# Linear attention and two FFNs on one core: the projected keys of pairs 9 to 13, with each head's rounded keys and their rest stacked on 128 rows

## The chip, the cores and the metric

One core of one Trainium2 chip runs the whole program. The metric is the device time of one execution in microseconds (us); a kernel's time is the median of its runs.

Engines are named as in the profile: PE is TensorE, PEld its weight load, DVE VectorE, ACT ScalarE, POOL GpSimd and SP SyncE, which here only issues transfers. SPq is SP's queue.

## The reference

```python
def phi(x):
    proj = np.einsum('bhsd,df->bhsf', x, w_phi)
    proj = proj - np.max(np.abs(proj), axis=-1, keepdims=True)
    return np.concatenate([np.exp(proj), np.exp(-proj)], axis=-1)
q_p, k_p = (phi(q), phi(k))
kv = np.einsum('bhsf,bhsd->bhfd', k_p, v)
z = np.sum(k_p, axis=2)
num = np.einsum('bhsf,bhfd->bhsd', q_p, kv)
den = np.einsum('bhsf,bhf->bhs', q_p, z)[..., None] + 1e-06
x = num / den                                # then heads side by side: 2304 x 512
h = x @ w_in1; x = np.maximum(0.01 * h, h) @ w_out1
h = x @ w_in2; x = (h / (1 + np.exp(-h))) @ w_out2
```

There are 4 x 8 = 32 heads, 576 positions each, head size 64 and 128 projected features. All data are fp32. The FFNs go from 512 to 2048 and back, for 2304 tokens.

## The kernel before, in words

**Pairs.** Two heads of one batch are one pair, so there are 16 pairs. A head has 64 rows, and a pair's raw keys (`kr`, 128 x 512) hold head 0 on rows 0 to 63 and head 1 on rows 64 to 127; the last 64 positions of both heads lie in `kt`. `full(i)` is true of pairs 0 to 7, which project in fp32. Pairs 8 to 15 take the split path: a value is rounded to the type F32R ("h"), what the rounding left is a second F32R value (the rest, "l"), and a product is built of passes with h and l parts. `sub(l, x, h)` is a DVE subtraction that gives the rest; all its uses carry line L271 in the profile.

**Steps of a split pair**, one function each: `s_split` rounds keys and queries; `s_pk(0)` and `s_pk(1)` project the keys, two chunks of 128 positions each into one PSUM bank; `s_pkt` projects the last 64 positions; `s_pq(a)` projects half of the queries; `s_eq(a)` and `k_exp` take the exponentials; `s_kv` sums keys times values (L389, L394) and splits the result into `KVH` and `KVL`; `num_split(a)` forms numerator and denominator (L576, copied to SBUF as `x` by ACT at L577), and sends the denominator through DRAM (`rec`) to be spread over 64 rows; `s_fin(a)` multiplies (L595) and splits the result for the FFN (L416).

A chunk of `s_pk` takes three passes of 256 columns, both heads side by side in the block-diagonal weights: L322 (rounded keys by rounded weights `BDH`), L323 (rest of keys by `BDH`), L324 (rounded keys by the weights' rest `BDL`). They add up in PSUM. `k_sub` then takes the largest magnitude of each group of 128 features (L299) and subtracts it (L300), both from PSUM.

**Around them** runs the first FFN for tokens that are ready: L851 multiplies into h, `g` (L857) and `gh` (L862) are its activation and rounding on ACT, `gl` the rest on DVE, and L882 multiplies them by `wo`, 12 passes a tile (8 with `gh`, 4 with `gl`). Jobs that prepare the second FFN's weights (`w7s`, `wst`) are put between.

**What sets the order.** Pairs 0 to 7 follow a table of times. A step of pair i from 8 on is emitted at 8 units times (i - 8) plus its entry in `OFF1`; `EARLY` gives hand-set times for pair 8 and a few steps of pair 9. Emission order gives priorities, by which a scheduler writes one list for each engine and each DMA queue; a list is worked off in order. PSUM tiles come from two pools of four banks each, `ps_a` and `ps_y`. All key and query projections, `kv`, `num` and h take a bank from `ps_a` in turn, so a pass waits until the bank's last tile has been read.

Of the kernel before, what the change touches and what calls it, by code (L numbers as in the profile page):

```python
# [102 lines left out]
EARLY = {  # L103
    (8, "lq"): (117.29,),
    (8, "lv"): (117.39,),
    (8, "sp"): (123.8, 127.98, 131.89, 133.51, 137.47, 140.31, 142.48, 147.66),
    (9, "lq"): (151.8,),
    (8, "pq0"): (161.92, 162.63),
    (8, "eq0"): (165.65, 167.79, 171.38, 172.55, 173.81),
# [12 lines left out]
def tile_linear_attention_ffn_ffn(ctx: ExitStack, tc: tile.TileContext, q, k, v, w_phi, w_in1, w_out1, w_in2, w_out2, out):  # L122


    nc = tc.nc
# [8 lines left out]
    HALF = S // 2  # L134
    WOB = 3
    RAWB = 3
    NFULL = 8
    ABUFS0 = dict(kr=2, kt=2, qr=3, va=3, ke=2, p=2, m=2, qh=2, x=2)
    ABUFS1 = dict(kr=2, kt=2, qr=2, va=1, qh=2, ql=2, x=2, d=2)
    NKV, NNUM = 128, 128  # L140
    MIN64, MAX64 = 2.0**-15, 122872.0

# [72 lines left out]
    WH = attc.tile([128, F], F32R, name="WH")  # L215
    BDH = attc.tile([128, 2, F], F32R, name="BDH")
    BDL = attc.tile([128, 2, F], F32R, name="BDL")

    def make_consts():
        for c in (slice(0, 2 * F), slice(2 * F, 3 * F + 128)):  # L220
# [32 lines left out]
    def load_qk(i):  # L253

        st = P[i]
        st["kr"] = at([128, S0], F32, "kr")
        st["kt"] = at([128, 128], F32, "kt")
        st["qr"] = at([128, S], F32, "qr")
        for c in (slice(0, 256), slice(256, S0)) if i == 0 else (slice(0, S0),):
            nc.sync.dma_start(st["kr"][:, c], k[i, :, c])  # L260
        nc.sync.dma_start(st["kt"], k[i, :, S0:])
        nc.sync.dma_start(st["qr"], q[i])

    def load_v(i):

# [4 lines left out]
    def sub(out_, x, h):  # L270
        return nc.vector.tensor_tensor(out_, x, h.bitcast(F32), op=ALU.subtract)  # L271
# [4 lines left out]
    def s_split(i):  # L276

        st = P[i]
        h, l = at([128, S0], F32R, "krh"), at([128, S0], F32R, "krl")
        nc.scalar.activation(h, st["kr"], AF.Copy)  # L280
        sub(l, st["kr"], h)
        st["krh"], st["krl"] = h, l
        qs = at([128, 2, S], F32R, "qs")
        for j in range(2):
            r, o = (slice(0, 64), slice(64, 128))[:: 1 - 2 * j]
            nc.scalar.activation(qs[r, j], st["qr"][r], AF.Copy)
            sub(qs[o, j], st["qr"][r], qs[r, j])
        st["qs"] = qs
        t = at([128, 128], F32R, "kth")
        nc.scalar.activation(t, st["kt"], AF.Copy)  # L290
        sub(t[64:128], st["kt"][64:128], t[64:128])
        st["kth"] = t

    def k_sub(i, pk, ng, g0):

        ke = P[i]["ke"]
        km = at([128, 4], F32, "km")
        src = pk[:, 0 : ng * F].rearrange("p (g f) -> p g f", f=F)
        nc.vector.tensor_reduce(km[:, 0:ng], src, op=ALU.max, axis=AX.X, apply_absolute_value=True)  # L299
        nc.vector.tensor_tensor(  # L300
            ke[:, g0 : g0 + ng, 0, :], src, km[:, 0:ng].unsqueeze(2).to_broadcast([128, ng, F]), op=ALU.subtract
        )

    def k_exp(i, g0, g1):
# [3 lines left out]
        nc.scalar.activation(e1, e0, AF.Exp, scale=-1.0)  # L308
        nc.scalar.activation(e0, e0, AF.Exp)

    def s_pk(c2):
        def f(i):
            st = P[i]
            if c2 == 0:
                st["ke"] = at([128, 9, 2, F], F32, "ke")
            pk = ps("a")
# [12 lines left out]
        return f  # L329
# [14 lines left out]
    def s_pq(a):  # L344

        def f(i):
            st = P[i]
            c0, n = part(i, a)
            p = at([128, 2 * n], F32, "p")
            st["p", a] = p  # L350
            pq = [ps("a"), ps("a")]
            cs = slice(c0, c0 + n)
            for j in range(2):
                nc.tensor.matmul(pq[j][:, 0:n], WH, st["qs"][:, j, cs], start=True, stop=False)
                nc.tensor.matmul(pq[j][:, 0:n], BDL[:, j], st["qs"][:, j, cs], start=False, stop=True)
# [210 lines left out]
    def num_split(i, a):  # L566
# [4 lines left out]
        for j in range(2):  # L571
            o = pn[j][:, 0:w]
            todo = [(s, g, m) for s in range(2) for g, m in (("KVH", "qh"), ("KVH", "ql"), ("KVL", "qh"))]
            for n, (s, g, m) in enumerate(todo):
                lhs = st[g][:, j, s].rearrange("p t d -> p (t d)")
# [37 lines left out]
    OFF1 = dict(lv=0.6, lq=-2.1250, sp=0.5, pq0=2.1172, pk0=4.0606, pk1=4.0616, pq1=4.7479, eq0=6.2094, pkt=5.1, kv=8.3898, num0=12.1423, eq1=13.9119, num1=14.457, fin0=FIN, fin1=FIN + 2.3)  # L613
# [729 lines left out]
def layout(inputs):  # L1343
# [16 lines left out]
    for j in range(2):  # L1360
        r = slice(64 * j, 64 * j + 64)
        va[:, r, 8 + j, D] = 1
        va[:, r, 8 + j, :D] = vp[:, j, S0:]

    bd = np.zeros((2 * D, 2 * w_phi.shape[1]), w_phi.dtype)
    for j in range(2):
        bd[D * j : D * j + D, w_phi.shape[1] * j : w_phi.shape[1] * (j + 1)] = w_phi
# [37 lines left out]
```

## Time and profile before

| | |
|---|---|
| median of 3 runs | 930.43 us (929.99 to 930.52) |
| profiled execution, its time | 930.31 us |
| profiled execution, its span | 928.5 us |
| PE busy | 922.0 us (99%) |
| DVE busy | 699.4 us (75%) |
| ACT busy | 600.8 us (65%) |
| POOL busy | 110.7 us (12%) |
| granted TensorE clock | 1.00 |

The span runs from the first to the last instruction that the profiler saw; 1.8 us of the execution's own time lie around it. Busy times of PE overlap with one another, because a pass starts before the one ahead has drained: what a pass costs is read from the start of one to the start of the next.

### The profile page before, as it was taken

Reading aid. Unit: us, or ns where it says so; the run is one execution under the profiler, and the core shown is the slowest. Engines: PE = TensorE matmul, PEld = TensorE weight load, DVE = VectorE, ACT = ScalarE, POOL = GpSimd, SP = SyncE. Lnnn points to the kernel's source line nnn. Section 1 sums busy time; section 2 is a strip of 40 time slices with the busy share of each in tenths; the row PEclk is TensorE's granted clock in tenths of the full one; section 3 lists DMA queues with packets and bytes.
Section 4 is the critical chain, followed back from the end, with each engine's and each line's share of the span. In section 5 each row is a group of like instructions: output and inputs, shape, how many; then the busy total and the mean of one; then the engine's idle time right before and its main releaser. Section 6 shows DMA issues by size and latency. Waiting matters only on the chain.

```text
span 928.5 us, 15779 instructions
## 1 busy us (share of the span) xinstructions
PE 922.0 (99%) x5382; PEld 873.1 (94%) x5382; DVE 699.4 (75%) x1425; ACT 600.8 (65%) x1240; POOL 110.7 (12%) x110
## 2 busy tenths in 40 slices
PE   8999999999999999999999999999999999999998
PEld 7999989999999999988988899999999999999998
DVE  6889999967777775799998888889755377553754
ACT  6888787876766665565767657766645456454553
POOL 4443000111211110101111111111000000000000
PEclk9999999999999999999999999999999999999999
DMA  6854474463434631569867899999898678977784
GB/s 230 277 187 171 139 253 158 158 209 122 124 122 131 210 107 59 203 248 335 314 238 268 296 371 364 381 360 353 280 364 269 221 243 289 317 259 227 245 271 162
DMA packets 99647, 221.40 MB, mean 238 GB/s; under 512 B 14896, under 2 KB 25264, under 8 KB 99568
## 3 DMA queue, kind: packets, MB, share of 16 engines
q1 hardware_dynamic: 90496, 187.79, 60.2%
q0 software_dynamic: 8640, 32.25, 9.1%
q8 instruction: 43, 0.70, 0.3%
q10 hardware_dynamic: 432, 0.36, 0.1%
q14 instruction: 36, 0.29, 0.1%
HBM read 173.10 MB, written 47.22 MB: 237 GB/s over the span
## 4 chain that ended last, share of the span: by engine, by line
PE 95%; ACT 1%; DVE 1%; DMA 1%; issue 1%; POOL 0%; SPq 0%; POOLq 0%; ACTq 0%; DVEq 0%
PE ps_y L1163 19%; PE ps_y L882 16%; PE ps_a L851 13%; PE ps_y L1080 10%; PE ps_a L1080 10%; PE ps_a L991 6%; PE ps_a L394 5%; PE ps_a L882 4%; PE ps_a L576 3%; PE ps_a L525 2%; PE ps_y L394 1%; PE ps_y L525 1%; DMA w7s<-wst 1%; PE ps_a L389 1%; DMA qr<-in_q_dram 0%
## 5 line engine op out<-in xcount | busy, mean ns | idle before, releaser
L1163 PE MATMUL ps_y<-gt,ws 128*128 128x384 f32 x1008 | 178.2, 337 | 0.0
L1163 PEld LDWEIGHTS ps_y<-gt,ws 128*128 128x128 f32 x1008 | 176.4, 188 | 1.0 <-DVE gt L271 0.7
L851 PE MATMUL ps_a<-xh,wi 128*128 128x462 f32 (+1 forms) x384 | 119.0, 373 | 0.0
L882 PE MATMUL ps_y<-gh,wo 128*128 128x462 f32 (+1 forms) x440 | 102.5, 372 | 0.0
L1080 PE MATMUL ps_y<-xs,ws 128*128 128x384 f32 x504 | 97.6, 338 | 0.0
L1080 PE MATMUL ps_a<-xs,ws 128*128 128x384 f32 x504 | 96.0, 338 | 0.0
L701 ACT ACTIVATE gt<-g 128x384 fp32r<-128x384 f32 x120 | 62.3, 524 | 46.1 <-PE ps_y L1163 44.8
L882 PEld LDWEIGHTS ps_y<-gh,wo 128*128 128x128 f32 x440 | 81.9, 188 | 9.0
L1080 PEld LDWEIGHTS ps_y<-xs,ws 128*128 128x128 f32 x504 | 89.5, 188 | 0.3
L1080 PEld LDWEIGHTS ps_a<-xs,ws 128*128 128x128 f32 x504 | 89.2, 188 | 0.0
L271 DVE TENSOR_TENSOR gt<-g,gt 128x384 fp32r<-128x384 f32 x120 | 65.1, 555 | 30.9 <-ACT gt L701 30.3
L851 PEld LDWEIGHTS ps_a<-xh,wi 128*128 128x128 f32 x384 | 72.1, 188 | 7.7
L851 PE MATMUL ps_a<-xl,wi 128*128 128x462 f32 (+1 forms) x192 | 71.4, 372 | 0.0
L1055 DVE TENSOR_TENSOR g<-ps_a,hs 128x384 f32<-128x384 f32 x36 | 20.0, 556 | 59.5 <-PE ps_a L1080 59.4
L359 POOL PARTITION_ALL_REDUCE m<-p x16 | 36.1, 2256 | 228.4 <-ACT p L357 176.1
L731 POOL DMA_DIRECT2D w7s<-wst x60 | 32.5, 542 | 233.2 <-DVE wst L271 162.7
L882 PE MATMUL ps_y<-gl,wo 128*128 128x462 f32 (+1 forms) x220 | 56.1, 374 | 0.0
L1051 ACT ACTIVATE hs<-ps_y 128x384 f32<-128x384 f32 x54 | 26.3, 487 | 35.7 <-DVE g L1055 33.2
L271 DVE TENSOR_TENSOR gl<-g,gh 128x462 fp32r<-128x462 f32 (+1 forms) x64 | 40.5, 633 | 10.8 <-ACT gh L862 9.6
L394 PE MATMUL ps_a<-va,ke 128*128 128x128 f32 x384 | 46.9, 275 | 0.0
L687 DVE CUSTOM_DVE_ANT_0 r<-t,r 128x1024 uint16<-128x1024 uint16 x64 | 45.3, 713 | 0.8
L882 PEld LDWEIGHTS ps_y<-gl,wo 128*128 128x128 f32 x220 | 41.0, 188 | 4.6
(215 smaller groups left out, 1956.6 us busy)
## 6 DMA issues: line engine op xcount, KB each, us to landing
ws<-w7s SPq DMA_DIRECT2D x336, 256.0 KB, 4.2
wo<-wos SPq DMA_DIRECT2D x46, 512.0 KB, 4.1
w7s<-wst POOLq DMA_DIRECT2D x45, 512.0 KB, 5.4
raw<-in_moe_w_out_dram SPq DMA_DIRECT2D x32, 512.0 KB, 5.0
rawi<-in_moe_w_in_dram SPq DMA_DIRECT2D x16, 512.0 KB, 6.3
wos<-wo SPq DMA_DIRECT2D x16, 512.0 KB, 2.9
raw<-in_moe_w_in_dram SPq DMA_DIRECT2D x16, 512.0 KB, 5.4
va<-in_v_dram SPq DMA_DIRECT2D x16, 325.0 KB, 4.8
```

Source lines behind the costliest of these rows:

```text
L271: return nc.vector.tensor_tensor(out_, x, h.bitcast(F32), op=ALU.subtract)
L359: nc.gpsimd.partition_all_reduce(m, p, 128, bass_isa.ReduceOp.absmax)
L394: nc.tensor.matmul(pv[:, s, j], ke[:, g, s, :], vf[:, w : w + NKV], start=False, stop=(j == 1 and c == 3), skip_group_check=True)
L525: nc.tensor.matmul(pb[:, w : w + NNUM], e[:, s, cs], KV[:, s, j], start=(s == 0), stop=(s == 1))
L687: nc.vector.tensor_tensor(r, t.bitcast(U32), r, op=ALU.add)
L701: nc.scalar.activation(h, f, AF.Copy)
L731: (nc.sync if seq else nc.gpsimd).dma_start(w7s[m_, p, :, i : i + m], o.bitcast(F32))
L851: nc.tensor.matmul(ph, a[:, kk, :], b_[:, kk, :], start=(m == 0), stop=(m == 3 * KD - 1))
L882: nc.tensor.matmul(Y[t][d][:, 0:n], a[:, ds_], b_, start=(c == 0 and m == 0), stop=(c == NC - 1 and m == 1), skip_group_check=True)
L991: nc.tensor.matmul(bank[b_], w1_of(p, wi_, a, kk), x1_of(xi, c, kk), start=(first and m == 0), stop=(m == 5), skip_group_check=True)
L1080: nc.tensor.matmul(bank[b_], w[:, a, kk], x[:, c, kk], start=(first and m == 0), stop=(m == 5), skip_group_check=True)
L1163: nc.tensor.matmul(bank[b_][db], w[:, a, db], t[:, c], start=(first and p_ == 0 and m == 0), stop=(p_ == NP - 1 and m == 2), skip_group_ch ...
```

## The change

For pairs 9 to 13 (`STACK`) the host lays out each head's keys twice, on rows 0 to 63 and again on rows 64 to 127, and the queries of pairs 8 to 15 likewise. One ACT copy rounds all 128 rows, and one DVE subtraction turns rows 64 to 127 into the rest. One pass over 128 rows then multiplies (rounded, rest) of one head and one chunk by `WB[:, 0:2]`, 256 columns: the first 128 are the rounded weights on both row halves and give the main sum, the others are the weights' rest on rows 0 to 63 and zero below, and give the correction. A chunk so takes two passes, one a head, and a bank of its own. ACT copies the correction half to SBUF, DVE adds the main half to it, and `k_sub` works on the sum in SBUF.

The other edits: queries are rounded for both heads at once; `KVH` and `KVL` are laid out by sign first and filled by two copies and two subtractions instead of four and four; `kr` and `qr` have one buffer instead of two; `pk0`, `pk1` and `pkt` have earlier entries in `OFF1`; `EARLY` loses two entries.

```diff
-    (8, "sp"): (123.8, 127.98, 131.89, 133.51, 137.47, 140.31, 142.48, 147.66),
+    (8, "sp"): (123.8, 127.98, 131.89, 137.47, 142.48, 147.66),
...
-    NFULL = 8
+    NFULL, STACK = 8, range(9, 14)
...
-    ABUFS1 = dict(kr=2, kt=2, qr=2, va=1, qh=2, ql=2, x=2, d=2)
+    ABUFS1 = dict(kr=1, kt=2, qr=1, va=1, qh=2, ql=2, x=2, d=2)
...
-        st["kr"] = at([128, S0], F32, "kr")
+        st["kr"] = at([128, S0] if i not in STACK else [128, 2, S0], F32, "kr")
...
-        st["qr"] = at([128, S], F32, "qr")
+        st["qr"] = at([128, S] if full(i) else [128, 2, S], F32, "qr")
...
+            nc.sync.dma_start(st["kr"], k[row : row + 2, :, 0:S0].rearrange("j p s -> p j s"))
...
-        h, l = at([128, S0], F32R, "krh"), at([128, S0], F32R, "krl")
-        nc.scalar.activation(h, st["kr"], AF.Copy)
-        sub(l, st["kr"], h)
-        st["krh"], st["krl"] = h, l
+        st["krs"] = at([128, 2, S0], F32R, "krs")
+        if i not in STACK:
+            h, l = st["krh"], st["krl"] = st["krs"][:, 0], st["krs"][:, 1]
+            nc.scalar.activation(h, st["kr"], AF.Copy)
+            sub(l, st["kr"], h)
+        else:
+            h = st["krs"]
+            nc.scalar.activation(h, st["kr"], AF.Copy)
+            sub(h[64:128], st["kr"][64:128], h[64:128])
         qs = at([128, 2, S], F32R, "qs")
-        for j in range(2):
-            r, o = (slice(0, 64), slice(64, 128))[:: 1 - 2 * j]
-            nc.scalar.activation(qs[r, j], st["qr"][r], AF.Copy)
-            sub(qs[o, j], st["qr"][r], qs[r, j])
+        nc.scalar.activation(qs, st["qr"], AF.Copy)
+        sub(qs[64:128], st["qr"][64:128], qs[64:128])
...
+    def stacked(i, c2):
+        st = P[i]
+        ke = st["ke"]
+        for c in (2 * c2, 2 * c2 + 1):
+            pk = ps("a").rearrange("p (t j f) -> p t j f", t=2, j=2)
+            for j in range(2):
+                nc.tensor.matmul(pk[:, :, j], st["krs"][:, j, c * 128 : (c + 1) * 128], WB[:, 0:2].rearrange("p t f -> p (t f)"), start=True, stop=True)
+            x, y = (ke[:, 2 * c : 2 * c + 2, t] for t in range(2))
+            nc.scalar.activation(y, pk[:, 1], AF.Copy)
+            nc.vector.tensor_tensor(x, pk[:, 0], y, op=ALU.add)
+        x = ke[:, 4 * c2 : 4 * c2 + 4, 0]
+        k_sub(i, x, 4, 4 * c2)
+        if c2 == 0:
+            k_exp(i, 0, 4)
...
-        for j in range(2):
-            kv_, z_ = pv[:, :, j, 0:D], pv[:, :, j, D : D + 1].to_broadcast([128, 2, D])
-            for slot, sr in ((j, kv_), (1 - j, z_)):
-                ops = nc.scalar.activation(h[:, j, :, slot, :], sr, AF.Copy), sub(l[:, j, :, slot, :], sr, h[:, j, :, slot, :])
+        z_ = pv[:, :, :, D : D + 1].to_broadcast([128, 2, 2, D])
+        for slots, sr in ((slice(0, 4, 3), pv[:, :, :, 0:D]), (slice(1, 3), z_)):
+            ho, lo = (x.rearrange("p s j t d -> p s (j t) d")[:, :, slots] for x in (h, l))
+            ops = nc.scalar.activation(ho, sr, AF.Copy), sub(lo, sr, ho)
...
-    OFF1 = dict(..., pk0=4.0606, pk1=4.0616, ..., pkt=5.1, ...)
+    OFF1 = dict(..., pk0=3.2, pk1=3.9, ..., pkt=4.6, ...)
```

In the order of TensorE's instructions, this stood at the key projection of pair 11 before (a tile's name, then what it is computed from; the group of three passes follows three more times, and then L576):

```order
L882 MATMUL ps_y<-gh,wo_2676 128x462 x8
L882 MATMUL ps_y<-gl,wo_2676 128x462 x4
L322 MATMUL ps_a<-BDH,krh 128x256
L323 MATMUL ps_a<-BDH,krl 128x256
L324 MATMUL ps_a<-BDL,krh 128x256
L322 MATMUL ps_a<-BDH,krh 128x256
```

And this stands there now (L908 is the line that was L882, L325 is the stacked pass):

```order
L908 MATMUL ps_y<-gl,wo_2670 128x462
L325 MATMUL ps_a<-WB,krs 128x2x128 x4
L908 MATMUL ps_y<-gl,wo_2670 128x462 x3
L325 MATMUL ps_a<-WB,krs 128x2x128 x4
L908 MATMUL ps_y<-gh,wo_2766 128x462 x8
```

Twelve passes became eight, the eight stand before the last passes of one FFN tile are done, and the 12 passes of the next FFN tile moved from behind the numerator (L576) to a place ahead of it (L602 now).

On ACT, the same place before, from the FFN's activation to the second copy of the numerator:

```order
L857 ACTIVATE g<-ps_a 128x462
L862 ACTIVATE gh<-g 128x462
L416 ACTIVATE xh<-x 128x288
L376 ACTIVATE e<-m 128x576
L280 ACTIVATE krh<-kr 128x512
L376 ACTIVATE m<-m 128x576
L577 ACTIVATE x<-ps_a 128x288
L308 ACTIVATE ke<-ke 128x4x128
L577 ACTIVATE x<-ps_a 128x288
```

And now (L442 was L416, L402 was L376, L603 was L577; L290 rounds the stacked keys of pair 12):

```order
L883 ACTIVATE g<-ps_a 128x462
L888 ACTIVATE gh<-g 128x462
L327 ACTIVATE ke<-ps_a 128x2x128 x2
L442 ACTIVATE xh<-x 128x288
L327 ACTIVATE ke<-ps_a 128x2x128 x2
L290 ACTIVATE krs<-kr 128x1024
L402 ACTIVATE e<-m 128x576
L402 ACTIVATE m<-m 128x576
L603 ACTIVATE x<-ps_a 128x288 x2
```

Four copies of corrections and a longer rounding now stand ahead of the two copies of the numerator, and the exponential of `ke` moved behind them.

## Rows read from the trace of the kernel before

**Rows 1.** The page, part 1: busy time, share of the span, instructions.

```profile
PE 922.0 (99%) x5382; PEld 873.1 (94%) x5382; DVE 699.4 (75%) x1425; ACT 600.8 (65%) x1240; POOL 110.7 (12%) x110
```

**Rows 2.** The page, part 4: the chain that ended last, by engine.

```profile
PE 95%; ACT 1%; DVE 1%; DMA 1%; issue 1%; POOL 0%; SPq 0%; POOLq 0%; ACTq 0%; DVEq 0%
```

**Rows 3.** Busy us (instructions) of PE, PEld, DVE, ACT, POOL; clock, DMA share, GB/s.

```profile
190.00:220.00 30.00, 30.00 (x187) 28.10 (x186) 22.47 (x45) 21.48 (x47) 4.38 (x2) 1.00 0.56 180
...
500.00:520.00 20.00, 20.00 (x97) 17.99 (x96) 16.88 (x35) 14.88 (x29) 3.79 (x7) 1.00 0.83 314
```

**Rows 4.** Timeline of PE at pair 10's key projection: start, length, what.

```profile
211.37 1.82 PE L882 MATMUL ps_y<-gh,wo 128*128 128x462 f32 x8
...
213.87 0.28 PE L322 MATMUL ps_a<-BDH,krh 128*128 128x256 f32 x1
...
215.27 0.30 PE L576 MATMUL ps_a<-qh,KVH 128*128 128x288 f32 x1
...
216.86 1.84 PE L882 MATMUL ps_y<-gh,wo 128*128 128x462 f32 x8
...
219.40 0.29 PE L354 MATMUL ps_a<-qs,WH 128*128 128x288 f32 x1
...
219.93 0.37 PE L851 MATMUL ps_a<-xh,wi 128*128 128x462 f32 x1
```

**Rows 5.** Timeline of ACT at the same place; idle time before in brackets.

```profile
215.51 0.45 ACT L416 ACTIVATE xh<-x 128x288 fp32r<-128x288 f32 x1 [1.55 <-DVE x L595]
...
216.89 0.61 ACT L280 ACTIVATE krh<-kr 128x512 fp32r<-128x512 f32 x1
217.41 0.67 ACT L376 ACTIVATE m<-m 128x576 f32<-128x576 f32 x1
217.99 0.39 ACT L577 ACTIVATE x<-ps_a 128x288 f32<-128x288 f32 x1
218.28 0.62 ACT L308 ACTIVATE ke<-ke 128x512 f32<-128x512 f32 x1
218.80 0.40 ACT L577 ACTIVATE x<-ps_a 128x288 f32<-128x288 f32 x1
```

**Rows 6.** Groups by line and shape: busy us, mean ns, idle before.

```profile
L271 DVE TENSOR_TENSOR krl<-kr,krh 128x512 fp32r<-128x512 f32 x8 | 5.5, 683 | 0.0
L280 ACT ACTIVATE krh<-kr 128x512 fp32r<-128x512 f32 x8 | 5.0, 622 | 1.6 <-issue 0.8 <-PE ps_a L324 0.8
L735 DVE TENSOR_TENSOR s<-r 128x256 f32<-128x256 f32 x16 | 6.7, 419 | 0.1
L473 ACT ACTIVATE p<-ps_a 128x256 f32<-128x256 f32 x15 | 5.4, 402 | 3.8 <-PE ps_y L462 3.0 <-DVE m L492 0.8
```

**Rows 7.** Timeline of PE at pair 10's key-value sums.

```profile
203.86 0.38 PE L389 MATMUL ps_a<-va,ke 128*128 128x130 f32 x2
204.08 1.95 PE L394 MATMUL ps_a<-va,ke 128*128 128x128 f32 x16
205.87 0.39 PE L389 MATMUL ps_a<-va,ke 128*128 128x130 f32 x2
```

**Rows 8.** Timelines of SPq and DVE, and median from issue to landing.

```profile
207.28 1.12 SPq L586 DMA_DIRECT2D x<-rec  x2
...
214.54 0.93 DVE L595 TENSOR_TENSOR x<-x 64x288 f32<-64x288 f32 x2
...
x<-rec SPq DMA_DIRECT2D x24, 72.0 KB, 2.6
```

**Rows 9.** Waits of PE's weight loads from 100 us on: total, times, longest.

```profile
PEld ps_y L882 <- ACT gh L701: 0.7, 1, 0.7
```

**Rows 10.** The chain that ended last, around that wait: start, length, what.

```profile
500.75 5.01 PE ps_a L991 x24
...
516.13 6.92 DMA w7s<-wst
...
528.61 1.93 PE ps_y L882 x8
```

More of the change, by code (lines that the diff above doesn't have):

```diff
@@ L214, in tile_linear_attention_ffn_ffn @@
     BDF, wraw, ident = wc[:, 0 : 2 * F].rearrange("p (j f) -> p j f", j=2), wc[:, 2 * F : 3 * F], wc[:, 3 * F :]
-    WH = attc.tile([128, F], F32R, name="WH")
     BDH = attc.tile([128, 2, F], F32R, name="BDH")
-    BDL = attc.tile([128, 2, F], F32R, name="BDL")
+    WB = attc.tile([128, 3, F], F32R, name="WB")
+    WH, BDL = WB[:, 0], WB[:, 1:3]
     def make_consts():
@@ L255, in load_qk @@
         st = P[i]
-        st["kr"] = at([128, S0], F32, "kr")
+        st["kr"] = at([128, S0] if i not in STACK else [128, 2, S0], F32, "kr")
         st["kt"] = at([128, 128], F32, "kt")
-        st["qr"] = at([128, S], F32, "qr")
[L259 to L262, printed above, removed]
+        st["qr"] = at([128, S] if full(i) else [128, 2, S], F32, "qr")
+        row = i + min(max(i - STACK[0], 0), len(STACK))
+        if i not in STACK:
+            for c in (slice(0, 256), slice(256, S0)) if i == 0 else (slice(0, S0),):
+                nc.sync.dma_start(st["kr"][:, c], k[row, :, c])
+        else:
+            nc.sync.dma_start(st["kr"], k[row : row + 2, :, 0:S0].rearrange("j p s -> p j s"))
+        nc.sync.dma_start(st["kt"], k[row, :, S0:])
+        nc.sync.dma_start(st["qr"], q[i] if full(i) else q[2 * i - NFULL : 2 * i - NFULL + 2].rearrange("j p s -> p j s"))
     def load_v(i):
@@ L278, in s_split @@
         st = P[i]
-        h, l = at([128, S0], F32R, "krh"), at([128, S0], F32R, "krl")
-        nc.scalar.activation(h, st["kr"], AF.Copy)
-        sub(l, st["kr"], h)
-        st["krh"], st["krl"] = h, l
+        st["krs"] = at([128, 2, S0], F32R, "krs")
+        if i not in STACK:
+            h, l = st["krh"], st["krl"] = st["krs"][:, 0], st["krs"][:, 1]
+            nc.scalar.activation(h, st["kr"], AF.Copy)
+            sub(l, st["kr"], h)
+        else:
+            h = st["krs"]
+            nc.scalar.activation(h, st["kr"], AF.Copy)
+            sub(h[64:128], st["kr"][64:128], h[64:128])
         qs = at([128, 2, S], F32R, "qs")
-        for j in range(2):
-            r, o = (slice(0, 64), slice(64, 128))[:: 1 - 2 * j]
-            nc.scalar.activation(qs[r, j], st["qr"][r], AF.Copy)
-            sub(qs[o, j], st["qr"][r], qs[r, j])
+        nc.scalar.activation(qs, st["qr"], AF.Copy)
+        sub(qs[64:128], st["qr"][64:128], qs[64:128])
         st["qs"] = qs
@@ L297, in k_sub @@
         km = at([128, 4], F32, "km")
-        src = pk[:, 0 : ng * F].rearrange("p (g f) -> p g f", f=F)
+        src = pk[:, 0 : ng * F].rearrange("p (g f) -> p g f", f=F) if len(pk.shape) == 2 else pk
         nc.vector.tensor_reduce(km[:, 0:ng], src, op=ALU.max, axis=AX.X, apply_absolute_value=True)
@@ L315, in f @@
                 st["ke"] = at([128, 9, 2, F], F32, "ke")
+            if i in STACK:
+                stacked(i, c2)
+                return
             pk = ps("a")
@@ L354, in f @@
                 nc.tensor.matmul(pq[j][:, 0:n], WH, st["qs"][:, j, cs], start=True, stop=False)
-                nc.tensor.matmul(pq[j][:, 0:n], BDL[:, j], st["qs"][:, j, cs], start=False, stop=True)
+                nc.tensor.matmul(pq[j][:, 0:n], BDL[:, 0], st["qs"][:, j, cs], start=False, stop=True)
             for j in range(2):
@@ L574, in num_split @@
             for n, (s, g, m) in enumerate(todo):
-                lhs = st[g][:, j, s].rearrange("p t d -> p (t d)")
+                lhs = st[g][:, s, j].rearrange("p t d -> p (t d)")
                 nc.tensor.matmul(o, lhs, st[m, a][:, s, j * w : (j + 1) * w], start=(n == 0), stop=(n == 5))
@@ L612, in tile_linear_attention_ffn_ffn @@
     FIN = 16
-    OFF1 = dict(lv=0.6, lq=-2.1250, sp=0.5, pq0=2.1172, pk0=4.0606, pk1=4.0616, pq1=4.7479, eq0=6.2094, pkt=5.1, kv=8.3898, num0=12.1423, eq1=13.9119, num1=14.457, fin0=FIN, fin1=FIN + 2.3)
+    OFF1 = dict(lv=0.6, lq=-2.1250, sp=0.5, pq0=2.1172, pk0=3.2, pk1=3.9, pq1=4.7479, eq0=6.2094, pkt=4.6, kv=8.3898, num0=12.1423, eq1=13.9119, num1=14.457, fin0=FIN, fin1=FIN + 2.3)
     seq = [(t, i, n_) for n_, ts in ORDER.items() for i, t in enumerate(ts)]
@@ L1363, in layout @@
         va[:, r, 8 + j, :D] = vp[:, j, S0:]
+    half = NP // 2
+    heads = qt[half:].reshape(half, 2, D, S)
+    qt = np.concatenate([qt[:half], np.concatenate([heads, heads], axis=2).reshape(2 * half, 2 * D, S)], axis=0)
+    a, b = half + 1, half + 6
+    head = kt[a:b, :, :S0].reshape(b - a, 2, 1, D, S0)
+    head = np.concatenate([head, head], axis=2).reshape(2 * (b - a), 2 * D, S0)
+    kt = np.concatenate([kt[:a], np.concatenate([head, np.repeat(kt[a:b, :, S0:], 2, axis=0)], axis=2), kt[b:]], axis=0)
     bd = np.zeros((2 * D, 2 * w_phi.shape[1]), w_phi.dtype)
```

## The prediction

> **What bounds the kernel now.** I read the busy times first: TensorE is at work for 922.0 us, 99% of the span [rows 1], and 95% of the chain that ended last is its own passes [rows 2]. A profile of this kind says that a pass taken away is time gained, unless a wait takes its place. So the next view is a stretch in which the changed pairs run. In 190 to 220 us PE is busy for all 30.00 us, while DVE has 22.47 us of work and ACT 21.48 [rows 3]: 7.5 and 8.5 us to spare. The granted clock is 1.00 there, the higher level of 2.4 GHz, and since PE does not pause, nothing in the rows speaks of a fall. Past 100 us the list of waits holds hardly anything: the longest wait is 0.7 us, once, at an FFN pass that needs `gh` [rows 9].
>
> **What is removed.** Pair 10's twelve key passes start at 213.87 us, and the pass behind them at 215.27 [rows 4]: 1.40 us for twelve, 0.117 us each. A stacked pass streams 256 columns with its own weights, as each of the old ones does, so I price it alike. A pair has eight in place of twelve and saves 4 x 0.117 = 0.467 us; five pairs save 20 x 0.117 = 2.33 us. No other pass is added or removed.
>
> One thing about the new pass is unlike the old: its output goes to two pieces of 128 columns with a gap between them. The row that bears on this is the first pass pair of `kv` (L389), which writes 2 x 65 columns to two places of a bank: two of them take 204.08 - 203.86 = 0.22 us, 0.11 each, and the sixteen that write 128 columns in one piece take 205.87 - 204.08 = 1.79 us, 0.112 each [rows 7]. The gap costs nothing there. The Trainium skill (PSUM — Partial Sum Buffer, Specifications) says otherwise: PSUM is written in lines of 8 bytes, and any non-contiguous access pattern slows matmuls significantly. Its rule gives no factor; a pass slowed by half would leave eight at the price of twelve, and the sum would be 930.3. This case's L389 row, 0.11 us against 0.112, disagrees with it, and I go by the row.
>
> **What is added on ACT and DVE.** Prices come from rows of 256 and 512 elements: ACT 402 and 622 ns, DVE 419 and 683 [rows 6]. A stacked pair adds four ACT copies of 256 (4 x 0.40 = 1.6 us) and four DVE additions of 256 (4 x 0.42 = 1.7 us). Going on at the same slope (0.22 and 0.264 us for 256 more), rounding 1024 key elements takes ACT 0.622 + 2 x 0.22 = 1.06 us for 0.62 before, and the rest takes DVE 0.683 + 2 x 0.264 = 1.21 for 0.68. Queries at once instead of twice, and `KVH`/`KVL` in two pieces instead of four, give back a few fixed costs, worth some tenths on each engine. That is about 1.7 us more for ACT and 1.7 for DVE a pair; even if two pairs' worth fell into one stretch of 30 us, 3.4 would go into 7.5 [rows 3]. As throughput it costs nothing; as delay it may, and that is the next part. No row shows the reduction of `ke` from SBUF instead of PSUM; it lies between free and the 0.68 of a 512-element DVE pass, and behind it only `ke`'s exponential waits, which `kv` wants only after another numerator and two more FFN tiles.
>
> **Transfers.** Queries of eight pairs and keys of five are loaded twice over. They are few and issued a whole pair ahead, with the DMA engines at a share of 0.56 [rows 3]. With one buffer a load waits until the pair before has been split; that is done by then, so I take nothing, and the bound is the rival "late finish" below.
>
> **The new tight place.** A pair's projection now takes four banks of `ps_a` in turn, and the bank that a later pass gets must have been read. I replayed pair 10 by its rows, with T the end of the last key pass. Before, T = 215.27. The two numerators' copies start at 217.99 and 218.80 on ACT, and h at 219.93 takes the second one's bank [rows 4, 5]: it is free at 218.80 + 0.40 = 219.20, which leaves 0.73 us.
>
> After: h's end is the fixed point (211.37), and T comes 0.47 us earlier against it. PE then does one FFN tile (219.40 - 216.86 = 2.54 us), the numerators (216.86 - 215.27 = 1.59), `pkt` (two passes of 128 columns, 2 x 0.112 by rows 7, 0.22) and the queries (219.93 - 219.40 = 0.53), so h begins at T + 4.88. The second numerator is done at T + 4.13, and its copy can start at about T + 4.25. ACT: the FFN copy L416 began at 215.51 when DVE let it, T + 0.24 before, hence T + 0.71 now, and takes 0.45. Behind it come two copies of corrections (0.58; a short copy is followed after 218.28 - 217.99 = 0.29), the rounding of 1024 (217.41 - 216.89 = 0.52 for 512, and 2 x 0.22 more, 0.96), and two exponentials (217.99 - 217.41 = 0.58 each). The first numerator's copy starts at T + 3.86 and ends at 4.25; the query pass that takes its bank begins at T + 4.62, 0.4 us later. The second's copy starts at T + 4.25 and ends at 4.64, and h comes 0.24 us later. So PE does not wait in the replay, but 0.73 us of slack became 0.2 to 0.4, in each of five pairs that are not all alike. I take 0.05 us a pair lost, 0.25 in all (bounds: nothing, and the 0.5 us a pair of the first rival).
>
> **Sum.** The profiled execution took 930.31 us (its span of 928.5 and 1.8 around it), 0.12 under the median of 930.43. 930.31 - 2.33 + 0.25 = 928.2; against the median, 928.3. I give 928.3. A measurement of this kernel can tell about 0.2% from no change, 1.86 us, so "faster" begins at 928.57, which my forecast only just passes.
>
> **The rivals.**
> *The banks eat it* (0.21). If ACT's work ahead of the numerators' copies is 0.5 us longer than replayed (a correction copy that waits for its pass, an exponential that waits for DVE's `m`), the stall at h is 0.26 a pair; at 0.71 us longer it is 0.47, the whole gain. 929.5 to 930.5: no change. For it speaks the slack of 0.2; against it, ACT's idle time ahead of L416, 1.55 us [rows 5], into which the first two correction copies fall.
>
> *Given back later* (0.13). From 500 us on DVE is busy 16.88 of 20 us [rows 3], and the one wait stands there: the chain leaves PE after 500.75 + 5.01, passes through ACT, DVE and a transfer of 6.92 us, and comes back at 528.61 [rows 10]. If that side does not start earlier when PE does, the 2.3 us come back as a longer wait: 929 to 930.5. Against it, the chain starts from PE, so it should move along.
>
> *Late finish, slower* (0.11). The load of the queries, which now waits for the pair before, can stand ahead of the denominator's transfers in SP's queue. Then the spread denominator comes late, DVE's L595 waits, with it ACT's L416, and behind that the correction copies, the rounding and the numerators' copies that PE waits for. Now the read is issued by 207.28 + 1.12 = 208.40, lands some 2.6 us later at 211.0, and L595 starts at 214.54: 3.5 us of room [rows 8]. Delays up to 3.5 us cost nothing, those beyond come out one for one, less the 0.24 at h; 3.5 + 0.24 + 0.47 = 4.2 us late takes the gain of a pair away, and half a us more than that in each of the five gives 930.3 + 5 x 0.5 = 932.8.
>
> *The pass does not shorten* (0.05). If the gap in the output counts, as the page's rule has it, eight passes cost twelve or more: 930.3 if slowed by half, 930.3 + 2.3 = 932.6 if doubled. L389 speaks against it.
>
> **How the numbers follow.** My forecast, with between nothing and 0.1 us lost a pair, has 0.50 and gives 927.9 to 928.6. From the cases: faster 0.51, same 0.36 (the banks, given back later, part of the others), slower 0.13. The range reaches from 927.6, a little more than the full gain (a stall of before that goes too), to 930.8, past the cases of no change; it leaves out the slower ones.
>
> **What would show it.** Right: eight starts 0.117 us apart where twelve stood, PE still at 30.00 us in each 30 between 190 and 310 us, and everything behind 310 us some 2 us earlier. The banks: gaps of some tenths at the first h pass or at the second query pass behind each numerator. Given back: equal starts from 530 us on, and a longer wait for `gh` before them. Late finish: idle time of DVE ahead of L621 (L595 before) that ends with the transfer from `rec`. Wrong altogether: starts 0.17 us apart or more at the stacked passes.

## The result and the profile after

The changed kernel takes 936.91 us (median of four runs, 935.73 to 937.79) against 930.21 for the kernel before; the ratio is 1.0069, 95% interval 1.0056 to 1.0082. It is slower by 6.7 us. The forecast was 928.3, with 0.13 on slower. The profiled execution is the fastest of the four: 935.73 us, span 933.6.

The page of the changed kernel, parts 1 and 4, answers to [rows 1, 2]:

```profile
PE 923.5 (99%) x5362; PEld 873.4 (94%) x5362; DVE 709.6 (76%) x1421; ACT 604.2 (65%) x1236; POOL 110.2 (12%) x110
...
PE 90%; DMA 4%; DVE 3%; ACT 2%; issue 1%; POOL 0%; SPq 0%; DVEq 0%; ACTq 0%
```

PE has 20 instructions fewer, as promised, and still 99%. But 4% of the chain that ended last is transfers now, where it was 1%. The windows (same columns as [rows 3]) say where:

```profile
190.00:220.00 30.00, 27.70 (x166) 25.29 (x164) 21.96 (x41) 19.92 (x45) 4.52 (x2) 1.00 0.71 224
...
220.00:222.00 2.00, 2.00 (x12) 2.00 (x13) 1.97 (x6) 1.97 (x4) 0.00 (x0) 0.80 0.13 51
222.00:224.00 2.00, 2.00 (x10) 1.95 (x9) 1.94 (x3) 2.00 (x6) 0.00 (x0) 0.50 0.01 0
224.00:226.00 2.00, 2.00 (x10) 1.77 (x9) 2.00 (x4) 2.00 (x6) 0.00 (x0) 0.85 0.66 179
```

In 190 to 220 us PE stands still for 2.30 of 30 us, and DVE and ACT are less busy than before, not more: all three wait for something else. The column behind POOL is the granted clock: 0.80, 0.50 and 0.85 in the three windows behind the pause. 0.50 is the lower level, 1.2 GHz. It costs 2 x (0.20 + 0.50 + 0.15) = 1.7 us. The timeline of PE shows the pause:

```profile
214.05 1.10 PE L325 MATMUL ps_a<-WB,krs 128*128 128x256 f32 x8
214.99 1.85 PE L908 MATMUL ps_y<-gh,wo 128*128 128x462 f32 x8
216.68 1.00 PE L908 MATMUL ps_y<-gl,wo 128*128 128x462 f32 x4
219.97 0.40 PE L602 MATMUL ps_a<-qh,KVH 128*128 128x288 f32 x1 [2.29 <-DVE ke L328]
```

Eight stacked passes take 214.99 - 214.05 = 0.94 us, 0.117 each: the saving is there at the price forecast, and the gap in their output costs nothing. The Trainium skill (PSUM — Partial Sum Buffer, Specifications) says that any non-contiguous access pattern slows matmuls significantly; for two pieces of 128 columns these rows do not agree. The last FFN pass starts near 217.3 and takes 0.21, and the numerator starts at 219.97: 2.45 us of nothing (2.29 by the profile, which ends the last pass at 217.68), ended by L328, DVE's addition of the correction. DVE at that time, and ACT's one row:

```profile
215.59 0.45 DVE L621 TENSOR_TENSOR x<-x 64x288 f32<-64x288 f32 x1 [0.31 <-DMA x<-rec]
218.34 0.46 DVE L621 TENSOR_TENSOR x<-x 64x288 f32<-64x288 f32 x1 [2.30 <-DMA x<-rec]
218.82 0.76 DVE L395 TENSOR_TENSOR m<-p,m 128x576 f32<-128x576 f32 x1
219.50 0.42 DVE L328 TENSOR_TENSOR ke<-ps_a,ke 128x256 f32<-128x256 f32 x1
...
218.83 0.44 ACT L442 ACTIVATE xh<-x 128x288 fp32r<-128x288 f32 x1 [3.95 <-DVE x L621]
```

The first correction was copied out by ACT at 214.49, so its addition could have run; it stands in DVE's list behind the finish L621 of an earlier pair, which waits 2.30 us for the denominators to come back from DRAM. The other three corrections stand on ACT behind L442, which waits for the same finish. In the kernel before, L595 stood at the same place and had its data [rows 8]; behind it L299 and L300 read two banks of keys too, but the numerators had the other two. Over the whole run the finish waits 10.2 us for this transfer, 2.4 before:

```profile
L621 DVE TENSOR_TENSOR x<-x 64x288 f32<-64x288 f32 x32 | 14.4, 450 | 10.7 <-DMA x<-rec 10.2
```

This finish belongs to the second half of a pair, and its denominators travel behind those of the first half. SP's queue, first of the kernel before, then of the changed kernel (start, time to issue, what); the read that belongs to this finish leaves at 207.28 before [rows 8] and at 212.18 after:

```profile
193.04 1.26 SPq L581 DMA_DIRECT2D e<-x  x2
...
195.02 1.11 SPq L260 DMA_DIRECT2D kr<-in_k_dram  x1
...
199.79 0.34 SPq L584 DMA_DIRECT2D rec<-e  x1
...
201.48 1.14 SPq L586 DMA_DIRECT2D x<-rec  x2
202.72 1.17 SPq L581 DMA_DIRECT2D e<-x  x2
205.89 0.33 SPq L584 DMA_DIRECT2D rec<-e  x1
```

```profile
193.90 0.62 SPq L607 DMA_DIRECT2D e<-x  x1
194.62 0.52 SPq L835 DMA_DIRECT2D wo<-wos  x1
195.97 0.38 SPq L264 DMA_DIRECT2D kr<-in_k_dram  x1
196.53 0.52 SPq L607 DMA_DIRECT2D e<-x  x1
...
204.20 0.34 SPq L610 DMA_DIRECT2D rec<-e  x1
205.60 1.15 SPq L612 DMA_DIRECT2D x<-rec  x2
206.84 1.18 SPq L607 DMA_DIRECT2D e<-x  x2
...
210.78 0.33 SPq L610 DMA_DIRECT2D rec<-e  x1
211.21 0.38 SPq L835 DMA_DIRECT2D wo<-wos  x1
212.18 1.13 SPq L612 DMA_DIRECT2D x<-rec  x2
```

And DVE of the changed kernel between them:

```profile
203.25 0.17 DVE L608 TENSOR_SCALAR e<-e 96x6 f32<-96x6 f32 x1 [1.54 <-DMA e<-x]
...
208.40 0.45 DVE L621 TENSOR_TENSOR x<-x 64x288 f32<-64x288 f32 x1 [2.10 <-DMA x<-rec]
...
209.55 0.46 DVE L621 TENSOR_TENSOR x<-x 64x288 f32<-64x288 f32 x1
...
210.57 0.19 DVE L609 RECIPROCAL e<-e 96x6 f32<-96x6 f32 x1
```

Before, the two small transfers of the first half's denominators left together, ahead of the keys' load, and the reciprocals were written at 199.79. After, the second leaves at 196.53, behind two loads of 512 KB. Not all of that is the queue: ACT had copied the numerator that it carries only at 194.85, against 192.80 before. It needs 6.6 us to land (the longest of these 1.1 KB transfers before needed 5.2), and the writing comes at 204.20: 4.4 us later. The second half inherits this. Its transfers stand in the queue behind the first half's read (205.60), its reciprocal stands in DVE's list behind the first half's finish, which waits 2.10 us for that read, and so its own read leaves 4.9 us later than before. The two transfers of this read then take 3.4 and 5.6 us to land, where the median is 2.7, and the last of them is what DVE waits for until 218.34.

The other waits of PE in 180 to 300 us (for what, us in total, times, longest), where the kernel before has none:

```profile
PE ps_a L602 <- DVE ke L328: 2.6, 2, 2.3
PE ps_a L877 <- DVE e L609: 1.2, 1, 1.2
PE ps_a L877 <- DVE ke L307: 0.4, 1, 0.4
```

L877 is h. It takes the bank of the last 64 keys, which L307 must have read, and L307 stands in DVE's list behind the denominators' L608 (253.84, 0.83 us here, where the median is 0.167) and behind all that the late finish at 244.52 had pushed back. PE busy in 180 to 310 us is 125.71 of 130 us, so pauses cost 4.3; with 1.7 of clock and 2.33 saved that is 3.7 of the 5.1 us by which the span grew; the rest is not assigned.

### The profile page after: what moved, and what is told of

It reads as the page before. It is cut to its first block, busy times and chain, and to the rows that moved or that the text cites. A ratio compares the mean times of both kernels' runs of the same rounds, so it can differ in the third digit from the quotient of the medians.

```text
span 933.6 us, 15731 instructions
## 1 busy us (share of the span) xinstructions
PE 923.5 (99%) x5362; PEld 873.4 (94%) x5362; DVE 709.6 (76%) x1421; ACT 604.2 (65%) x1236; POOL 110.2 (12%) x110
## 4 chain that ended last, share of the span: by engine, by line
PE 90%; DMA 4%; DVE 3%; ACT 2%; issue 1%; POOL 0%; SPq 0%; DVEq 0%; ACTq 0%
PE ps_y L1189 19%; PE ps_y L908 15%; PE ps_a L877 11%; PE ps_y L1106 10%; PE ps_a L1106 10%; PE ps_a L1017 8%; PE ps_a L908 4%; PE ps_a L420 4%; PE ps_a L551 2%; PE ps_a L602 2%; DMA x<-rec 2%; PE ps_y L420 1%; DMA e<-x 1%; DMA rec<-e 1%; PE ps_y L551 1%
## 5 line engine op out<-in xcount | busy, mean ns | idle before, releaser
L877 PE MATMUL ps_a<-xh,wi 128*128 128x462 f32 (+1 forms) x384 | 119.8, 375 | 1.6 <-DVE e L609 1.2
L908 PE MATMUL ps_y<-gh,wo 128*128 128x462 f32 (+1 forms) x440 | 104.3, 374 | 0.0
L908 PEld LDWEIGHTS ps_y<-gh,wo 128*128 128x128 f32 x440 | 81.2, 188 | 8.8 <-ACT gh L888 0.2
L877 PEld LDWEIGHTS ps_a<-xh,wi 128*128 128x128 f32 x384 | 72.7, 189 | 10.1 <-issue 1.4
L877 PE MATMUL ps_a<-xl,wi 128*128 128x462 f32 (+1 forms) x192 | 71.7, 373 | 0.0
L275 DVE TENSOR_TENSOR gl<-g,gh 128x462 fp32r<-128x462 f32 (+1 forms) x64 | 40.8, 638 | 20.4 <-ACT gh L888 19.4
L908 PE MATMUL ps_y<-gl,wo 128*128 128x462 f32 (+1 forms) x220 | 56.2, 373 | 0.0
L908 PEld LDWEIGHTS ps_y<-gl,wo 128*128 128x128 f32 x220 | 41.0, 188 | 4.6
```

Of the source, the lines that this page charges most:

```text
L877: nc.tensor.matmul(ph, a[:, kk, :], b_[:, kk, :], start=(m == 0), stop=(m == 3 * KD - 1))
L908: nc.tensor.matmul(Y[t][d][:, 0:n], a[:, ds_], b_, start=(c == 0 and m == 0), stop=(c == NC - 1 and m == 1), skip_group_check=True)
```

## The experiments

My theory after the result, A: a stacked pair takes four banks, each next pass hangs on a reader of one of them, and the readers stand behind late transfers. Rivals: B, the doubled loads; C, the earlier offsets; D, lateness that no single order takes away. Every comparison is with the kernel before on the same chip; its medians lay between 930.28 and 930.46.

**Without stacking, with all the rest.** `STACK = ()`, keys loaded once.

> All edits of the change stay (queries loaded twice over and rounded at once, KVH and KVL in two pieces, one buffer for kr and qr, the earlier offsets), but no pair is stacked, so TensorE saves nothing. Theory A, that the numerator waits for a bank that only stacking ties to DVE's additions: TensorE shows no gap over 0.3 us between 180 and 300 us, the clock stays at 1.00, and the time is that of the kernel before, 930 us within 0.6, even if the finish is still late on DVE. Rival B, that the doubled loads or the held-up transfer queue hurt by themselves: 932 us or more, with gaps at 200 to 280 us.

931.17 us, ratio 1.0009 (0.9999 to 1.0018), not to be told from the kernel before. PE is without a pause:

```profile
180.00:310.00 130.00, 129.98 (x812) 121.83 (x811) 92.51 (x176) 87.77 (x181) 22.90 (x10) 1.00 0.51 158
```

So the doubled queries, the merged `KVH` and `KVL`, the single buffers and the earlier offsets cost nothing that shows.

**Stacking with none of the rest** (but `kr` has one buffer): queries are loaded once, `KVH` and `KVL` are in four pieces. Two of the edits, against the changed kernel:

```diff
-    ABUFS1 = dict(kr=1, kt=2, qr=1, ...)
+    ABUFS1 = dict(kr=1, kt=2, qr=2, ...)
-    OFF1 = dict(..., pk0=3.2, pk1=3.9, ..., pkt=4.6, ...)
+    OFF1 = dict(..., pk0=4.0606, pk1=4.0616, ..., pkt=5.1, ...)
```

> Stacking alone on the kernel before: the old offsets, the queries loaded once with two buffers, KVH and KVL in four pieces; kr keeps one buffer, since two doubled ones do not fit. 20 passes fewer, 2.3 us. Theory A: the coupling is still there, but less stands ahead of the denominator's transfers; if the finish comes in time, 928 us, if it comes late, the gaps ahead of the numerators stay and the time is 932 us or more. Rival B, doubled bytes of the queries: near 928.5. Rival C, that the earlier offsets of the key projection cost the time: near 928.5 as well.

937.25 us, ratio 1.0073 (1.0058 to 1.0088): as slow as the whole change. Rival C falls, and B as far as queries go. The waits are others, though; most of it is that of h for the last keys, the second one of above:

```profile
PE ps_a L879 <- DVE ke L309: 5.1, 4, 2.0
PE ps_a L382 <- DVE ke L330: 0.7, 1, 0.7
PE ps_a L327 <- ACT g L885: 0.6, 1, 0.6
```

**Loads of kt and qr behind the denominators' read**, by an order without a wait.

```diff
...
+            for ins in nc.cur_bb.bb.instructions[seen:]:
+                tc.add_manual_dep(ins, reads[-1].name, nosync, reason="order")
```

> The changed kernel, but the loads of kt and qr stand behind the denominator's read on the transfer queue, as in the kernel before. Theory A, the held-up queue as the cause of the late finish: DVE's wait for the read at 216 to 218 us and at 243 us vanishes, TensorE has no gap there, the clock does not fall, 928 to 929.5 us. Rival B, doubled bytes that slow the small transfers: the same waits stay within 0.7 us, 934 us or more.

944.09 us, ratio 1.0154: far slower, where 928 to 929.5 was expected. The numerators' pause shrank (0.5 us of waits for additions, 2.6 in the change), but the queries came too late for their own passes:

```profile
PE ps_a L387 <- DVE qs L282: 7.4, 2, 4.1
PE ps_a L609 <- DVE ke L335: 0.5, 2, 0.2
```

This is not the order of the kernel before either: there the loads of qr and kt left at 200.57 and 201.09, ahead of the read at 201.48. Behind the read they are too late, with one buffer here and, as a run below shows, with two.

**The finish emitted four units later** (`FIN = 20`).

> The changed kernel with the finish emitted 4 units later (20 and 22.3 instead of 16 and 18.3), behind the key projection of the pair two on, so that DVE's additions need not stand behind a multiplication that waits for a transfer. Theory A: gaps ahead of the numerators of 0.5 us at most in all, 928 to 929.5 us, whatever the transfers do. If the numerators' wait has another cause than the finish ahead of the additions, 933 us or more.

945.46 us, ratio 1.0166. No pass waits for an addition any more, as expected, but in 180 to 310 us the query pass waits 1.7 us for ACT's copy of the numerator, and between 640 and 660 us the second FFN waits for its activation and its weights (2.0, 1.8 and 1.3 us). That the late finish pushed these back is likely, but not shown. The waits are as expected, the time (928 to 929.5) is not.

**Order on DVE.** Three runs aim at DVE's list: the first puts the finish behind additions, the second the denominators behind the last keys, the third does both. For the first and the third `fin1` of pairs 8 to 11 is emitted at 20, for the second and the third `pkt` at 4.1; the lists of the other engines shift a little with that.

```diff
...
+                    tc.add_manual_dep(mul.ins, adds[i + 2].ins.name, ..., reason="order")    # finish behind additions
...
+            tc.add_manual_dep(den.ins, pkts[i + 1].name, ..., reason="order")    # denominators behind the last keys
```

> The changed kernel, with the second half's finish (L621 of fin1) of pairs 8 to 11 put behind the additions of the pair two on in DVE's list; no wait is taken away. Theory A in two parts: (i) the numerator waits for a bank that an addition frees, and the addition stands behind a finish that waits for a transfer: 2.46 and 0.47 us, and about 2.2 us of half clock behind the first; (ii) the second h waits for the bank of the last 64 keys, whose subtraction stands behind the denominators' transfer: 1.40 and 0.52 us. This run takes (i) away alone: 931 to 933 us, the gaps of (ii) still there. If the lateness goes elsewhere instead (rival D): within 1.5 us of 936.9.

> The changed kernel, with the denominators' first addition (L608) of a pair's first half put behind the subtraction of the next pair's last 64 keys, which for that is emitted a little earlier (4.1 instead of 4.6). It takes (ii) away alone: 1.9 us less, 934.5 to 936 us, the gaps ahead of the numerators still there. Rival D: within 0.8 us of 936.9, or slower, since the denominators come later and with them the finish.

> Both orders. Theory A: no gap over 0.5 us between 180 and 300 us, the clock at 1.00, 928.5 to 930.5 us: the 2.3 us of removed passes show at last. Rival D: 933 us or more, with gaps at other places.

933.56 us (ten executions, 930.54 to 936.61), 932.92 (930.70 to 935.86) and 935.22. Each order alone takes away the wait it was made for, and gains 3.4 and 4.0 us on the change. The second gained more than expected (934.5 to 936), and took away more: of the 2.6 us at the numerators 0.6 were left, beside a new 1.2 at the last keys. Together they gain only 1.7. The waits of the first and of the third in 180 to 300 us:

```profile
PE ps_a L881 <- DVE e L611: 0.7, 1, 0.7
PE ps_a L382 <- ACT x L605: 0.6, 1, 0.6
PE ps_a L881 <- DVE ke L307: 0.5, 1, 0.5
```

```profile
PE ps_a L383 <- ACT x L606: 2.2, 2, 1.9
PE ps_a L884 <- DVE ke L307: 0.9, 3, 0.4
```

The query pass (L382, L383) waits for ACT's copy of the numerator: the place that the prediction had found tight. So A's first half holds (the waits are where it says), and D's as well: a wait that is taken away at one bank comes back at the next.

**Without the correction.** Stacked passes of 128 columns with the rounded weights alone, two chunks in a bank; the correction of pairs 9 to 13 is left out, and with it ACT's copies and DVE's additions.

> Stacking as in the change, loads, buffers and offsets too, but the correction (rounded keys by the weights' rest) of pairs 9 to 13 is left out: eight passes of 128 columns a pair, two chunks in one bank, no copy on ACT and no addition on DVE, the maximum and subtraction straight from PSUM. TensorE is let off 12 x 0.117 - 8 x 0.06 = 0.92 us a pair, 4.6 in all. If the four banks and their release by DVE are the cause (theory A): no gap over 0.5 us between 180 and 300 us and 925 to 927 us. If the doubled loads of keys with one buffer, or the longer rounding, are the cause (rival B): gaps at 200 to 280 us stay, 929 us or more.

930.75 us (929.74 to 934.55). My price for the passes was wrong: four take 213.18 - 212.79 = 0.39 us in this trace, 0.10 each and not 0.06, so 0.6 us a pair is saved and not 0.92, 3.1 in all. Waits of 1.9 us are left, in three pieces, at h. With the extra banks and the additions gone, most of the loss is gone, but not all: 3.1 saved would have given 927.3, so 3.4 us are still lost, and by the expectation's own mark (929 or more, waits left) this is rival B, loads or rounding. The longer rounding (1.22 us on DVE) still stands ahead of the subtraction that h waits for; how much of the 3.4 us it makes is not shown.

**ACT frees all banks.** One ACT copy of 512 elements empties a bank, and DVE adds in SBUF; then the same with queries loaded once; then queries loaded once and kt and qr ordered behind the read; then both.

```diff
-            nc.scalar.activation(y, pk[:, 1], AF.Copy)
-            nc.vector.tensor_tensor(x, pk[:, 0], y, op=ALU.add)
+            nc.scalar.activation(ke[:, 2 * c : 2 * c + 2].rearrange("p j t f -> p t j f"), pk, AF.Copy)
...
```

> The changed kernel, but ACT copies both halves of a chunk out of its bank (512 elements instead of 256), and one addition of DVE in SBUF makes the sum for two chunks. The banks of the key passes are then freed by ACT alone, and DVE's additions can stand behind a late finish without holding a bank. If the tie to DVE is what costs the time: the numerators' gap of 2.46 us and the half clock behind it go, 931 to 933.5 us, though ACT has 0.9 us a pair more to do. If it is that four banks are taken at all, whoever frees them: as slow as the change or slower, 936 us or more, with the waits now on ACT.

> The same, and the queries are loaded once, with two buffers and four short pieces of rounding as before the change, so that 295 KB a pair less are read and no load of queries waits for the pair before. If the loads matter for the small transfers: at least 1 us under the run with ACT's copy alone. If not: within 1 us of it.

> The changed kernel with the queries loaded once and two buffers, and with the loads of kt and qr behind the denominators' read in the transfer queue, as in the kernel before; the additions stay on DVE. It takes away both the held-up queue and the late queries that the run with this order alone showed (3.4 and 4.3 us of waits for qs). If the held-up queue is what makes the finish late: no numerator gap over 0.5 us, 929 to 932 us. If the finish is late in any case: 934 us or more.

> Both: queries loaded once, the old order of loads, and all banks of the key passes freed by ACT. If every tie named so far is real: 928.5 to 931 us, at best 1.5 us under the kernel before. If four banks a projection are too many whatever frees them: 932 us or more.

936.61, 934.61, 945.00 and 938.83 us. In the first, no pass waits for DVE, and one waits 2.5 us for ACT (`PE ps_a L379 <- ACT x L602`): as slow as the change, as expected if four banks are too many whoever frees them. Loading the queries once helps by 2.0 us, more than the 1 us set as the mark beforehand; but the intervals of the two ratios overlap (1.0044 to 1.0079, 1.0025 to 1.0057), and buffers and rounding of the queries changed with it, so that is open. The two with the order of loads still wait for `qs` (6.2 and 3.1 us in all), though they have the second buffer that was expected to cure it.

**Four banks on the kernel before.** Three passes a chunk, nothing stacked, but a bank for each chunk.

```diff
-                o = pk[:, u * 2 * F : (u + 1) * 2 * F]
+                if u and 9 <= i < 14:
+                    pk2 = ps("a")
+                o = pk2[:, 0 : 2 * F] if u and 9 <= i < 14 else pk[:, u * 2 * F : (u + 1) * 2 * F]
...
```

> The kernel before, with three passes a chunk and nothing stacked, but in pairs 9 to 13 each chunk takes a bank of its own, and the maximum and subtraction are done for each chunk, 256 elements at a time (0.6 us of DVE a pair more). No pass is saved, no load, buffer or offset changed. If four banks a projection are the cause: gaps ahead of the numerators, the queries or h between 180 and 310 us, 932 to 936 us. If it is the stacking's longer rounding, its loads or its additions: 930.4 us within 0.8, no gap over 0.3 us.

933.22 us, ratio 1.0032 (1.0020 to 1.0044). PE at pair 10:

```profile
214.27 0.28 PE L326 MATMUL ps_a<-BDL,krh 128*128 128x256 f32 x1
215.48 0.36 PE L324 MATMUL ps_a<-BDH,krh 128*128 128x256 f32 x1 [0.94 <-DVE KVL L271]
...
219.57 0.37 PE L582 MATMUL ps_a<-qh,KVH 128*128 128x288 f32 x1 [0.62 <-DVE ke L300]
...
221.03 0.37 PE L582 MATMUL ps_a<-qh,KVH 128*128 128x288 f32 x1 [0.43 <-DVE ke L300]
```

The third chunk waits for the bank of `kv`, the numerators for the banks of the chunks. Nothing but the number of banks (and 0.6 us of DVE a pair) was edited, and it costs 2.8 us. The scheduler's order follows: the FFN tile moved ahead of the numerators, as in the change. This is the clearest of the runs. It also shows that the denominators can be late with nothing stacked and no load doubled: the second small transfer leaves at 195.08, among others behind a load of keys of the old size, and the writing comes at 203.53, almost as late as in the change. (The Trainium skill, Perfetto Trace Analysis, Optimization Strategy, says that a bubble which repeats in a stretch can mean too little PSUM for the next tile; these rows agree.)

**Two stacked pairs alone**, 12 and 13, then 9 and 10.

> The change, with pairs 12 and 13 alone stacked. 8 passes fewer, 0.93 us. In the changed kernel the gaps at pairs 9 to 11 are 2.46, 0.47 and 1.40 us and the half clock, those at 12 and 13 are 0.52 us and some tenths. If the cost sits where DVE has the weight jobs and late finishes between (pairs 10 and 11), this one is 929.5 to 930.3 us, a little under the kernel before; if each stacked pair costs more than the 0.47 us that it saves, 930.8 to 932.

> The change, with pairs 9 and 10 alone stacked: also 8 passes fewer. By the gaps of the changed kernel the numerators of pair 10's neighbourhood wait here (2.46 us and 2.2 of half clock), so 933 to 936 us. If the cost is the same for each stacked pair, 1.3 us net: about 932.9 for two pairs, and the run with pairs 12 and 13 is as slow.

931.30 us, ratio 1.0012 (1.0003 to 1.0021), and 933.34, ratio 1.0032 (1.0017 to 1.0046). Both a little slower than the kernel before, the first at the edge of what can be told. Neither is worth it: against the 0.93 us saved stand 1.8 us lost in the first and 3.8 in the second (the difference to 930.46, and the saving). The cost is not the same for each pair. Part of it may be the other edits': with all of them and nothing stacked the time was 931.17, and on top of that pairs 12 and 13 come out even.

**The keys' load alone behind the denominators' read**, in the changed kernel; and **the added bytes alone**, as copies to DRAM, in the kernel before.

> The changed kernel; only the doubled load of the keys (524 KB) is put behind the denominators' read in the transfer queue, where in the change it stands between the two small transfers of the denominators. The keys are needed some 20 us later, so this lateness costs nothing. If that load holds up the small transfer (6.6 us to landing in the change, 5.2 at most before): the denominators come 1.5 us or more earlier, the numerators' gap of 2.46 us shrinks under 1.5 and with it the half clock, 932 to 935 us. If the lateness has other causes: within 1 us of 936.9.

> The kernel before, and beside each load of keys (pairs 9 to 13) and of queries (pairs 8 to 15) the same bytes are copied once more to a spare place in DRAM, on the same queue. Nothing waits for these copies. If the added transfers alone delay the small ones enough to matter: 931.5 us or more. If only a kernel whose banks hang on the finish feels it: 930.4 us within 0.6.

932.89 us, ratio 1.0028 (1.0009 to 1.0047), and 930.00, ratio 0.9998 (0.9988 to 1.0008). The second says nothing of the bytes: nothing held its copies to the loads beside which they were written, and in its trace the copies of keys leave between 4.5 and 19.4 us, those of queries by 120.5, where the change's doubled loads of keys leave between 129.6 and 249.8 (160 to 340 us moved 26.95 MB, as in the kernel before; 29.30 in the change). So rival B stays open for the doubled keys; for the queries, doubled without harm in the run without stacking, it falls. The first run gains 4.0 us on the change. With it the finish has its data and PE does not pause ahead of the numerators (DVE and PE of that run):

```profile
215.35 0.95 DVE L628 TENSOR_TENSOR x<-x 64x288 f32<-64x288 f32 x2
```

```profile
217.27 1.00 PE L915 MATMUL ps_y<-gl,wo 128*128 128x462 f32 x4
218.11 0.30 PE L608 MATMUL ps_a<-qh,KVH 128*128 128x288 f32 x1
...
221.13 0.48 PE L884 MATMUL ps_a<-xh,wi 128*128 128x462 f32 x1 [0.50 <-ACT x L609]
```

The read of this finish leaves at 211.88, only 0.3 us earlier than in the change, but its transfers land in 3.4 us at most, not 5.6. The edit also let the scheduler move DVE's 1.22 us of the keys' rounding from 221.90 to 211.62, so it is not one change alone, and what the load's place is worth by itself is not shown. What is left is the wait of h for ACT's copy, 0.50 us here, and 1.2 us at 448 us, where a pass of a later stage waits for ACT.

## Why the prediction was wrong

**What bounds the kernel, and the saving.** Right: 20 passes at 0.117 us, measured 0.117.

**What is added on ACT and DVE.** Right in its prices. DVE's rounding of 1024 measured 1.22 us (1.21 forecast), ACT's 1.06 (1.06), an addition 0.417, a copy 0.383. In 190 to 220 us both engines were less busy than before, because they waited too.

**The new tight place.** This step failed. The replay followed only ACT's copies of the numerators, because they were the tight ones before. It took the banks of the four chunks, which the numerators, the last keys and the first query pass now get, to be free in time, and it took the finish to begin when it did before. Both were wrong: the numerator's bank is freed by L328, which stands behind the finish, and the finish was late: 2.45 us of pause where the replay had none. The tight place that I found at h was real (0.50 us of wait there in the run with the keys' load moved), but it is one of several of that kind, and each showed up as the wait in some run: DVE's reading of the keys' banks ahead of the numerators (the change, and four banks on the kernel before), the last keys' subtraction ahead of h (stacking alone), ACT's copies (both orders on DVE, and ACT freeing the banks).

**Transfers.** This step failed too: "I take nothing". It looked at whether the moved loads come in time for their own use, and not at what they delay. In SP's queue, worked off in order, they stood between the denominators' two transfers. How much of the lateness is theirs is open, since four banks on the kernel before split the two transfers as well.

**The rivals.** "Late finish, slower" (0.11) was the mechanism, in its main lines: a load in front of the denominators in SP's queue, then DVE's wait for `rec`. It named the queries' load; the load between the two transfers was the keys'. It had the delay reach PE through ACT's list, with 3.5 us of room; it reached PE through a bank that DVE frees, with ACT's other three corrections held by the same finish. It had no term for the clock, 1.7 us. "The banks eat it" (0.21) named the right resource, but priced only ACT's delay; four banks on the kernel before show 2.8 us for it, more than the 2.33 saved. "Given back later" and "the pass does not shorten" were not what happened in the change.

**The sum as the runs give it.** Against its own saving the change lost 936.9 - 930.2 + 2.3 = 9.0 us. Four banks alone cost about 2.8 of them (933.22 against 930.46), which already turns 2.3 saved into 0.5 lost. The late finish, taken out of DVE's way by order, gives back 3.4, the half clock in it; moving the keys' load, with what moved along, 4.0. These overlap and cannot be added: both orders on DVE together gave back only 1.7. And with two banks and no additions, but with all the loads and the longer rounding, 3.4 were still lost. That the several waits give way to one another, I could show; how the 9.0 us split among banks, rounding and late denominators, and what the doubled keys add, not.

## What to carry to other kernels

Before passes are traded for PSUM banks, write down for each bank who takes it next and who frees it, on every engine, and replay all of them, not only the one that was tight before: an engine with 25% idle time can still be the one that TensorE waits for, if what frees the bank stands in its list behind a wait for a transfer. A load that is moved on an in-order queue has to be checked against the small transfers behind it, and not only against when its own data are wanted. Where taking away one wait brings up another, look at the count of buffers rather than at the next order. And look in the trace whether a test's added work ran where it was meant to: the copies that were to stand for the doubled loads of keys left more than 100 us ahead of them.

## What the runs showed of the hardware

A pause of TensorE can cost more than its length: behind the 2.45 us in the changed kernel the granted clock was 0.80, 0.50 and 0.85 in three windows of 2 us, and full again after 226 us. Not each pause does that: the longest single wait of the run in which ACT frees the banks was 2.5 us, and its clock stayed at 1.00.

A small transfer can be slow for its size: two reads of 72 KB, issued at 212.2 and 212.7 us behind a 512 KB load, took 3.4 and 5.6 us to land, where the median of such reads is 2.7. In the run with the keys' load moved the same two reads, also behind a 512 KB load, took 3.4 at most; what made the difference is not shown.

Some of these kernels vary more: ten executions of the run with the finish behind the additions spread over 6.1 us, 25 of the kernel before in the same comparison over 1.9. Why is not shown.
